# A fused Fourier mixing and hardswish MLP kernel: one difference of VectorE placed behind a block's last output sum, and the second batch's inverse stage in four units of three tiles on another list of steps

## The chip, the cores and the metric

The kernel runs on one core of one Trainium2 chip. The metric is the device time of one execution in microseconds (us). The median of three executions before the change is 2656.8 us (2656.7 to 2656.96). The engines are called as the profile calls them: PE is TensorE's matmuls and PEld its weight loads, DVE is VectorE, ACT is ScalarE, POOL is GpSimd, SP is the engine that issues most DMAs.

## The reference

```python
x: (8, 3008, 256)    filt_r, filt_i: (1505, 256)    w_in: (256, 2048)    w_out: (2048, 256)

X = np.fft.rfft(x, axis=1)
Y = X * (filt_r + 1j * filt_i)[None, :, :]
y = np.fft.irfft(Y, n=3008, axis=1).astype(np.float32)      # mixing along the sequence

t = y.reshape(8 * 3008, 256)                                # 24064 tokens
h = t @ w_in
g = h * np.clip(h + 3.0, 0.0, 6.0) / 6.0                    # hardswish
out = g @ w_out
```

All of it is in float32.

## The kernel before

**Two parts, woven together.** The MLP runs over 47 blocks (`NBLK`) of 512 tokens. A block has eight pairs (`NP`), each for 256 of the 2048 hidden channels. The Fourier mixing runs per batch, as matmuls with tables: 3008 is 47 times 64, and the transform goes through a stage over the 47 (`a_unit`), a stage over the 64 (`b_unit`), the product with the filter (`f_unit`, then the sums in `y_unit`), an inverse stage over the 64 (`bi_unit` or `bi3_unit`), and an inverse stage over the 47 (`n_unit`, `n_five`), which writes the tokens of the coming blocks. Between the stages the data goes through DRAM: `z_tmp` after the first, `g_tmp` after the inverse one, written by `z_store`, `z6_store`, `g_store` and `g3_store` and read back by `t2_load` and `t4_load`. Batch 0 is done ahead; batches 1 to 7 are woven into the MLP of the batch before.

**Steps and the plan.** The loop at the end of the kernel goes through steps i = 8k + p, for block k and pair p. In step i it emits the up half of item i and the down half of item i - 1. The dictionary `plan` says which units of the mixing are emitted in which step, at one of three places: place 0 right behind `up_1`, place 1 behind the first `hswish`, place 2 at the step's end. `at` chooses: `a_unit`, `b_unit`, `bi_unit`, `n_unit` and `n_five` go to place 0 (`EARLY`), `bi3_unit` and `a6_unit` to place 1, all else, `f_unit`, `y_unit` and the stores among them, to place 2. Within one place the order is that of the calls of `at`: those of `n_five` come before those of `b_unit`, and a batch's `y_unit` calls before its `f_unit` calls. The function `places` gives the steps: for batch 1 four lists written out by hand, for the others a regular pattern. The kernel is scheduled by hand: every engine works through its instructions in the order in which this loop emits them.

**A step of the MLP.** The products are done with seven multiplications in place of eight, both up and down. Up (line 764): `up_1` has three products of 256 columns, `up_2` two, `up_3` and `up_5` one each; every matmul shows twice in the profile, as two passes. They go to the PSUM tiles `al` and `be`; ScalarE copies parts out, and VectorE adds them to the two halves of h (`up_2b` line 790, `up_3` line 795). The product of `up_5` goes into the part of `al` that line 795 has read. ScalarE makes relu (line 809), and `hswish` on VectorE (line 814) makes g. The second `hswish` of an item is emitted in the next step, in `g_sums`, ahead of lines 821 and 822, which make the sums G1, G3 and G2. `g_last` (line 827) makes G4. Down (line 843): products 1; then 2 and 4; then 5 and 6; then 7 and 3, each of 128-column matmuls, eight of them in the profile for two products. G4 is used by product 3 alone, the last of a step; 2 and 4 use what the second `hswish` makes, 5 uses G1, 6 G2 and 7 G3.

**Where `g_last` stands.** It comes right behind `g_sums`, or, where `late(i)` holds, behind `up_3`. `late(i)` holds for the second and third step of each block (i % 8 in 1, 2), and where the step before had a heavy unit in the plan (`f_unit`, `y_unit`, sums, `bi3_unit`, `n_five`).

**A block's end.** The eight pairs accumulate in four PSUM banks, `po0` to `po3`. Products 7 and 3 share bank 3, in two halves, and product 7 of pair 0 opens the bank for a new block. In the step of a block's last pair (i % 8 = 0), `out_1` copies a bank on ScalarE, and `out_2` (line 909) and `out_3` (line 914) on VectorE follow, `out_3` behind products 7 and 3 and ahead of place 2. In the next step (i % 8 = 1, the new block's pair 0), `out_4` (lines 918 and 919, and line 920 on GpSimd) and `out_5` (line 923) finish the output. `out_5` reads product 3's half of bank 3; then `store` sends the block out.

**The inverse stage over the 64.** A batch has twelve y tiles (`NU`). `y_unit` makes each one from two products of `f_unit`, which reads a `psF` bank that `b_unit` filled. For batch 1 `b_unit` fills one bank for each y tile; for later batches it fills two at once. `bi_unit` (line 583) takes two y tiles: four matmuls of 512 columns into two `psF` banks, two copies by ScalarE into the tile `t3`, two DMAs on GpSimd's queue (`g_store`, line 630). `bi3_unit` (line 599) takes three: twelve matmuls of 256 columns into two `psF` banks and the PSUM tile `be`; two copies by VectorE (2 and 510 elements, lines 601 and 603) and two by ScalarE (line 602, and line 610 at the end of the step) into `t3`; four DMAs (`g3_store`, lines 615 and 618). Batch 1 uses `bi_unit`, batches 2 to 7 `bi3_unit`.

**Buffers.** `psF` has two banks, shared by `b_unit`, `bi_unit`, `bi3_unit`, `n_unit`, `n_five` (which takes both) and `a6_unit`; `t3` has one buffer, which `a6_unit`, the next batch's first stage, uses too; y tiles three (`yp`), the products of `f_unit` two (`sp`). Five-column chunks of the last stage, `n_five` with 80 matmuls (line 704) and two copies by ScalarE (line 686), stand in steps 17 and 25; its copies set off seven sums of GpSimd (line 760) for the coming block.

Of the kernel before, what the change touches and what calls it, by code (L numbers as in the profile page):

```python
# [39 lines left out]
NB = HC // XC  # L40
# [142 lines left out]
def kernel(  # L183
# [452 lines left out]
    for b in range(B):  # L636
# [4 lines left out]
        n = 0  # L641
# [146 lines left out]
    def up_2b(k, p):  # L788
        al, be, s, s5 = st["up"]
        nc.vector.tensor_tensor(out=st["h"][0].rearrange("p (a n) -> p a n", a=2), in0=be, in1=s, op=ALU.add)  # L790
# [26 lines left out]
    def g_sums(k, p):  # L817
        hswish(k, p, 1)
        g = st["g", k, p]
        v = nc.vector  # L820
        v.tensor_tensor(out=g[:, G1, :], in0=g[:, G3, :], in1=g[:, G22, :], op=ALU.add)  # L821
        v.tensor_tensor(out=g[:, G3:G2 + 1:2, :], in0=g[:, G3:G1 + 1, :],  # L822
                        in1=g[:, G11:G11 + 1, :].broadcast_to([P, 2, 256]), op=ALU.subtract)

    def g_last(k, p):
        g = st["g", k, p]
        nc.vector.tensor_tensor(out=g[:, G4, :], in0=g[:, G12, :], in1=g[:, G2, :], op=ALU.subtract)  # L827
# [42 lines left out]
    def plain_up(p):  # L870
        st["g", 0, p] = gp.tile([P, 7, 256], FP32, name="g")
        st["h"] = [psU.tile([P, 512], FP32, name=n) for n in ("al", "be")]
        for i in range(2):
            for d in range(2):
                nc.tensor.matmul(st["h"][i], w_in[p][:, 2 * d + i, :], xn[:, d, :, 0:PAIRS], start=d == 0, stop=d == 1)  # L875
            relu(i)
            hswish(0, p, i)

    def plain_down(p, tokens=(0, 1)):
        g = st["g", 0, p]  # L880
        if p == 0:
            st["po", 0] = [psO.tile([P, 2, 2, P], FP32, name="po%d" % i) for i in range(2)]
        for t in tokens:
            for u in range(2):
                for i, a in ((0, G11), (1, G12)):
                    nc.tensor.matmul(st["po", 0][t][:, u, :, :].rearrange("p a m -> p (a m)"), g[:, a + t, ts(u, P)],  # L886
                                     w_out[p][:, 2 * i:2 * i + 2, :].rearrange("p j m -> p (j m)"),
                                     start=p == 0 and u == 0 and i == 0, stop=p == NP - 1, skip_group_check=True)
# [14 lines left out]
    def o_at(k, t, d):  # L903
        return st["o", k][0][:, t, :, ts(d, P)]
# [17 lines left out]
    def out_5(k):  # L922
        nc.vector.tensor_tensor(out=o_at(k, 0, 1), in0=st.pop(("po", k))[3][:, 1, :, :], in1=o_at(k, 0, 1), op=ALU.add)
        store(k)
# [20 lines left out]
    def store(k):  # L945
        o = st["o", k][0]
        nc.sync.dma_start(o_d[ds(k * PAIRS, PAIRS)].rearrange("(u p) d -> p u d", p=P), o[:, 1, :, :])
        for u, p, m, b_, j, a in runs(k):
            for h in range(1 if j else 2):
                nc.sync.dma_start(raw(out, b_ * N + row(j, h, a), [[NC * D, m], [1, D]]), o[p:p + m, h, u, :])  # L950
        for b_, r, j, m, na in BACK.get(k, ()):
            to, half = out.offset + (b_ * N + N - j) * D, D // 2
            a0, a1 = ([[D, m], [-NC * D, na], [1, D]], [[NA * D, m], [D, na], [1, D]]) if m > 1 else (
                [[half, 2], [-NC * D, na], [1, half]], [[half, 2], [D, na], [1, half]])
            nc.sync.dma_start(bass.AP(tensor=out.tensor, offset=to, ap=a0),
                              bass.AP(tensor=o_d.tensor, offset=o_d.offset + r * D, ap=a1))
# [18 lines left out]
    def at(step, fn, *a):  # L975
        plan.setdefault((step, 0 if fn in EARLY else 1 if fn in (w_scale, bi3_unit, a6_unit) else 2), []).append((fn, a))

    with tc.manual_schedule():
# [160 lines left out]

        def places(n):  # L1140
            if n == 1:
                return (list(range(2, NB + 2)), [12, 13, 15, 18, 19, 20, 22, 23, 26, 27, 28, 30],
                        [14, 15, 16, 19, 21, 22, 24, 25, 27, 29, 30, 31], [16, 21, 24, 29, 31, 32])
            k = first[n] * NP
            a_at = [k - 7 * NP + i for i in A_AT]
            f_at, y_at, bi_at = ([k - (5 - 2 * r) * NP + i for r in range(2) for i in p]
                                 for p in ((2, 3, 6, 7, 12, 13), (4, 5, 10, 11, 14, 15), (11, 17)))
            return a_at, f_at, y_at, bi_at
# [4 lines left out]
        for n in range(1, B):  # L1153
            a_at, f_at, y_at, bi_at = places(n)
            for c, s in enumerate(a_at):
                at(s, a_unit if n == 1 else a6_unit, n, c)
                at(s, a_sums if n == 1 else a6_sums, n, c)
                at(s, *((z_store, n, c, nc.sync) if n == 1 else (z6_store, n, c)))
                if c >= (3 if n == 1 else 2):
                    at(max(a_at[c - 3 + (n > 1)], s - 6), x_load, n, c)  # L1160
                elif n > 1:
                    at(max(prev[-1 if n == 2 else c - 2], s - 6), x_load, n, c)
            for c in range(NT):
                s = f_at[2 * (c - TB) + (n == 1)] + 1 if c >= TB else a_at[-1] + 1
                at(s, t2_load, n, c)
                s = f_at[2 * (c - FB) + 1] + 1 if c >= FB else a_at[-1 if n > 1 else 3] + 1
                at(s, table_load, n, c)
            for i in range(NU):
                if i % 2 == 0 or n == 1:
                    at(f_at[i], b_unit, n, i)  # L1170
                if n == 1 and i % 2 == 0:
                    at(bi_at[i // 2], bi_unit, n, i)
                    at(bi_at[i // 2], g_store, n, i)
                if n > 1 and i % 3 == 0:
                    at(bi_at[i // 3], bi3_unit, n, i)
                    at(bi_at[i // 3], g3_store, n, i)
                at(y_at[i], y_unit, n, i)
            for i in range(NU):
                at(f_at[i], f_unit, n, i)
            prev = a_at  # L1180
# [5 lines left out]
        def late(i):  # L1186
            return i % NP in (1, 2) or any(fn in HEAVY for place in range(3) for fn, a in plan.get((i - 1, place), ()))

        items = [(k, p) for k in range(NBLK) for p in range(NP)]
        for i in range(len(items) + 1):  # L1190
            up = i < len(items)
            k, p = items[min(i, len(items) - 1)]
            dn = i > 0
            kd, pd = items[i - 1]
            def do(place):
                for fn, a in plan.get((i, place), ()):
                    fn(*a)

            if k == 0:
                plain_up(p)  # L1200
                do(0)
                if dn:
                    plain_down(pd)
                do(1)
                do(2)
                continue
            if not up:
                last_down()
                break
            up_1(k, p)  # L1210
            ends = k == LAST and p == NP - 1
            do(0)
            last_plain = dn and kd == 0
            dn = dn and kd > 0
            if dn:
                g_sums(kd, pd)
                if not late(i):
                    g_last(kd, pd)
                down(kd, pd, 1)
            if up:  # L1220
                up_2(k, p)
            if dn and pd == 0 and kd > 1:
                out_4(kd - 1)
            if up:
                up_2b(k, p)
            if dn:
                down(kd, pd, 2, 4)
                if pd == NP - 1:
                    out_1(kd)
            if up:  # L1230
                up_3(k, p)
                if dn and late(i):
                    g_last(kd, pd)
            if dn:
                down(kd, pd, 5, 6)
            if up:
                up_4(k, p)
            if ends:
                out_1(k)
            if last_plain:  # L1240
                plain_down(pd, (0,))
            if dn and pd == 0 and kd > 1:
                out_5(kd - 1)
            if up:
                hswish(k, p, 0)
                do(1)
            if up:
                up_5(k, p)
            bi3_copies()
            if last_plain:  # L1250
                plain_down(pd, (1,))
                plain_out()
            if dn:
                if pd == NP - 1 or ends:
                    out_2(kd)
                down(kd, pd, 7, 3)
                if pd == NP - 1 or ends:
                    out_3(kd)
            do(2)
# [30 lines left out]
```

## Time and profile before

| | |
|---|---|
| median of 3 executions | 2656.8 us |
| the profiled execution | 2656.55 us, its span 2654.7 us |
| TensorE clock granted | 0.999 on average |
| DMA, mean over the span | 75 GB/s |
| an ordinary step without mixing work | 6.15 us |
| the same with a `b_unit` of batch 1 (line 548) | 7.01 us |

The step starts below are those of the first `up_1` matmul of each step in TensorE's timeline (us from the start of the span). They cover the steps in which batch 1 has its middle stages; batch 1's `a_unit` calls come before, and batch 2's first `a6_unit` comes in step 36.

| step | 12 | 16 | 17 | 18 | 20 | 21 | 24 | 25 | 29 | 31 | 32 | 33 | 34 | 35 |
|---|---|---|---|---|---|---|---|---|---|---|---|---|---|---|
| start | 157.80 | 184.98 | 193.89 | 201.74 | 215.76 | 223.11 | 245.17 | 252.86 | 282.19 | 296.89 | 305.80 | 313.16 | 319.50 | 325.65 |

How to read what follows: a line of the timeline has the start, the length, the engine, the line of the kernel, the operation, what it writes and reads, and how many instructions are merged in it; in brackets is how long the engine was idle before it and what ended that. A group or a wait counts all such instructions of the span. Ends of matmuls are modelled, their starts are not.

### The profile page before, as it was taken

The numbers are of one execution on the slowest core, as the hardware profiler recorded it, in microseconds if no ns is written. First come the engines' busy times: TensorE is split into PE (matmuls) and PEld (weight loads), VectorE is DVE, ScalarE is ACT, GpSimd is POOL, SyncE is SP. The second block draws the span as 40 slices with busy tenths as digits, with TensorE's granted clock in tenths as the row PEclk, the third lists the DMA queues.
The fourth block names the chain that finished last, engine by engine and source line by source line (L and its number), as shares of the span: only waits on it lengthen the run. The fifth ranks groups of instructions, "written<-read, shape, count | busy, mean of one in ns | idle before, by whom it ended". The sixth has DMA issues, their size and how long they took to land.

```text
span 2654.7 us, 54856 instructions
## 1 busy us (share of the span) xinstructions
PE 2638.6 (99%) x21872; PEld 2334.1 (88%) x21872; DVE 2038.2 (77%) x3602; ACT 1298.6 (49%) x2682; POOL 484.3 (18%) x707
## 2 busy tenths in 40 slices
PE   8999999999999999999999999999999999999999
PEld 6688888889889898898988988889888888999998
DVE  7878767887678876788767887688877878766666
ACT  4554454444544444444444544545445444454554
POOL 2242021120211102121021210211112120111110
PEclk9999999999999999999999999999999999999999
DMA  9732234112241133411333112331223321110000
GB/s 248 219 92 71 72 84 115 52 32 82 79 116 52 32 85 81 111 52 36 80 88 104 52 37 80 89 103 52 56 61 88 103 56 48 48 43 22 19 20 25
DMA packets 130646, 198.29 MB, mean 75 GB/s; under 512 B 21538, under 2 KB 97408, under 8 KB 130198
## 3 DMA queue, kind: packets, MB, share of 16 engines
q1 hardware_dynamic: 115165, 150.12, 20.7%
q0 software_dynamic: 14656, 44.16, 6.0%
q8 instruction: 173, 2.83, 0.5%
q14 instruction: 83, 0.68, 0.1%
q10 hardware_dynamic: 569, 0.50, 0.1%
HBM read 122.43 MB, written 83.98 MB: 78 GB/s over the span
## 4 chain that ended last, share of the span: by engine, by line
PE 97%; DVE 2%; DMA 1%; issue 0%; ACT 0%; SPq 0%; POOL 0%; POOLq 0%; DVEq 0%
PE po L843 43%; PE al L764 24%; PE be L764 18%; PE psn L704 2%; PE psf L539 1%; PE psf L480 1%; PE po L886 1%; PE be L599 1%; PE psf L599 1%; PE be L480 1%; PE psf L583 0%; DMA w_all<-in_x_dram 0%; PE al L875 0%; PE be L875 0%; DVE g L814 0%; PE po L548 0%
## 5 line engine op out<-in xcount | busy, mean ns | idle before, releaser
L843 PEld LDWEIGHTS po<-w_all,g 128*128 128x128 f32 x10276 | 1366.4, 191 | 121.1 <-issue 20.3
L843 PE MATMUL po<-w_all,g 128*128 128x128 f32 x10276 | 1396.7, 276 | 1.2 <-DVE g L814 0.6
L809 ACT ACTIVATE r<-h,half_c 128x512 f32<-128x512 f32 x736 | 531.0, 721 | 334.1 <-DVE h L790 322.0
L764 PE MATMUL al<-xt,w_all 128*128 128x256 f32 x2208 | 659.7, 381 | 0.1
L814 DVE SCALAR_TENSOR_TENSOR g<-r,h 128x512 f32<-128x512 f32 x736 | 530.1, 720 | 159.8 <-ACT r L809 144.7
L764 PE MATMUL be<-xt,w_all 128*128 128x256 f32 x1472 | 437.8, 379 | 0.0
L790 DVE TENSOR_TENSOR h<-be,s 128x512 f32<-128x512 f32 x368 | 253.8, 690 | 157.3 <-PE be L764 148.6
L764 PEld LDWEIGHTS al<-xt,w_all 128*128 128x128 f32 x2208 | 335.5, 192 | 1.0 <-issue 0.5
L764 PEld LDWEIGHTS be<-xt,w_all 128*128 128x128 f32 x1472 | 279.8, 190 | 37.8
L760 POOL TENSOR_TENSOR xt<-xn 128x256 f32<-128x256 f32 x184 | 135.9, 757 | 876.7 <-ACT xn L686 842.6
L804 ACT ACTIVATE h<-al 128x256 f32<-128x256 f32 x368 | 141.0, 383 | 299.8 <-PE al L764 299.8
L795 DVE TENSOR_TENSOR h<-al,s 128x256 f32<-128x256 f32 x368 | 156.3, 425 | 157.4 <-PE al L764 154.1
L822 DVE TENSOR_TENSOR g<-g 128x512 f32<-128x512 f32 x367 | 261.3, 712 | 12.6
L785 ACT ACTIVATE s<-al 128x256 f32<-128x256 f32 x368 | 141.1, 383 | 211.9 <-PE al L764 210.4
L764 PE MATMUL al<-xn,w_all 128*128 128x256 f32 x736 | 226.1, 389 | 0.0
L776 ACT ACTIVATE s<-be 128x256 f32<-128x256 f32 x368 | 141.1, 383 | 172.2 <-PE be L764 172.2
L764 PE MATMUL be<-xn,w_all 128*128 128x256 f32 x736 | 218.9, 379 | 0.0
L821 DVE TENSOR_TENSOR g<-g 128x256 f32<-128x256 f32 x367 | 167.5, 456 | 12.6
L775 ACT ACTIVATE s<-al 128x256 f32<-128x256 f32 x368 | 140.8, 383 | 71.7 <-PE al L764 71.7
L764 PEld LDWEIGHTS be<-xn,w_all 128*128 128x128 f32 x736 | 139.9, 190 | 18.9
L827 DVE TENSOR_TENSOR g<-g 128x256 f32<-128x256 f32 x367 | 154.6, 421 | 2.5
L920 POOL TENSOR_TENSOR o<-p,o 128x256 f32<-128x256 f32 x46 | 36.8, 799 | 602.8 <-DVE o L918 557.4
(171 smaller groups left out, 1933.5 us busy)
## 6 DMA issues: line engine op xcount, KB each, us to landing
t<-g_tmp SPq DMA_DIRECT2D x184, 120.0 KB
t<-z_tmp SPq DMA_DIRECT2D x42, 512.0 KB
g_tmp<-t POOLq DMA_DIRECT2D x72, 256.0 KB, 5.5
z_tmp<-t POOLq DMA_DIRECT2D x120, 144.0 KB, 3.4
o_tmp<-o SPq DMA_DIRECT2D x46, 256.0 KB
xs<-in_x_dram SPq DMA_DIRECT2D x60, 192.0 KB
ft<-in_filt_r_dram SPq DMA_DIRECT2D x168, 64.0 KB
ft<-in_filt_i_dram SPq DMA_DIRECT2D x168, 64.0 KB
```

The lines of the kernel that those rows point to most:

```text
L764: nc.tensor.matmul(ps, w_in[p][:, w, :], x, start=start, stop=stop, skip_group_check=True)
L776: nc.scalar.activation(out=s5, in_=be[:, 1, :], func=AXT.Copy)
L785: nc.scalar.activation(out=s[:, 1, :], in_=al, func=AXT.Copy)
L790: nc.vector.tensor_tensor(out=st["h"][0].rearrange("p (a n) -> p a n", a=2), in0=be, in1=s, op=ALU.add)
L795: nc.vector.tensor_tensor(out=st["h"][1][:, 256:512], in0=al, in1=s5, op=ALU.add)
L804: nc.scalar.activation(out=st["h"][1][:, 0:256], in_=al, func=AXT.Copy)
L809: nc.scalar.activation(out=r, in_=st["h"][i], func=AXT.Relu, bias=half_c, scale=1.0 / 6.0)
L814: nc.vector.scalar_tensor_tensor(out=st["g", k, p][:, o:o + 2, :].rearrange("p a n -> p (a n)"), in0=st["r", i], scalar=1.0, in1=st["h"][i ...
L821: v.tensor_tensor(out=g[:, G1, :], in0=g[:, G3, :], in1=g[:, G22, :], op=ALU.add)
L822: v.tensor_tensor(out=g[:, G3:G2 + 1:2, :], in0=g[:, G3:G1 + 1, :], in1=g[:, G11:G11 + 1, :].broadcast_to([P, 2, 256]), op=ALU.subtract)
L827: nc.vector.tensor_tensor(out=g[:, G4, :], in0=g[:, G12, :], in1=g[:, G2, :], op=ALU.subtract)
L843: nc.tensor.matmul(st["po", k][bank][:, part, u, :], g[:, a, ts(u, P)], w_out[p][:, w, :], start=(p == 0 and n in OPENS and u == 0), stop= ...
```

## The change

It has two parts. In the loop, for every pair 0 of a block from the third on (`pd == 0 and kd > 1`), `g_last` is emitted behind `out_5` and no longer behind `up_3`: on VectorE lines 827 and 923 change places. And for batch 1 the six `bi_unit` calls with their `g_store` become four of `bi3_unit` with `g3_store`, so that the stage's matmuls come at place 1 of a step; the lists of steps for `f_unit` (and `b_unit`, which shares its list), `y_unit` and the inverse units are other ones. `f_unit` and `y_unit` no longer share a step, three steps have two `y_unit` calls, and the last inverse unit is in step 34 where it was in 32. The steps of `t2_load` and `table_load` follow from the list of `f_unit`.

```diff
         def places(n):
             if n == 1:
-                return (list(range(2, NB + 2)), [12, 13, 15, 18, 19, 20, 22, 23, 26, 27, 28, 30],
-                        [14, 15, 16, 19, 21, 22, 24, 25, 27, 29, 30, 31], [16, 21, 24, 29, 31, 32])
+                return (list(range(2, NB + 2)), [12, 13, 16, 17, 19, 21, 22, 24, 27, 28, 30, 32],
+                        [14, 15, 18, 20, 20, 23, 26, 26, 29, 31, 31, 33], [20, 26, 31, 34])
...
             for i in range(NU):
                 if i % 2 == 0 or n == 1:
                     at(f_at[i], b_unit, n, i)
-                if n == 1 and i % 2 == 0:
-                    at(bi_at[i // 2], bi_unit, n, i)
-                    at(bi_at[i // 2], g_store, n, i)
-                if n > 1 and i % 3 == 0:
+                if i % 3 == 0:
                     at(bi_at[i // 3], bi3_unit, n, i)
                     at(bi_at[i // 3], g3_store, n, i)
                 at(y_at[i], y_unit, n, i)
...
             if up:
                 up_3(k, p)
-                if dn and late(i):
+                if dn and late(i) and not (pd == 0 and kd > 1):
                     g_last(kd, pd)
...
             if dn and pd == 0 and kd > 1:
                 out_5(kd - 1)
+                g_last(kd, pd)
             if up:
                 hswish(k, p, 0)
                 do(1)
```

`bi3_unit` and its helpers, which batch 1 now calls as the others do:

```python
    def bi3_unit(b, i):
        ys = [st.pop(("y", b, i + v)) for v in range(3)]
        c = psU.tile([P, 512], FP32, name="be")
        banks = [psF.tile([P, 512], FP32, name="psf", tag="f") for ri in range(2)]
        t = t3p.tile([P, 3, 2, D], FP32, name="t3")
...
        nc.scalar.activation(out=to[1], in_=banks[1], func=AXT.Copy)
        nc.vector.tensor_copy(out=to[2][:, 2:512], in_=c[:, 2:512])
...
    def g3_store(b, i):
        t = st.pop(("t3", b, i))
        for v in range(2):
            nc.gpsimd.dma_start(g_d[b, :, :, ds(2 * (i + v), 2), :].rearrange("c ri u d -> c ri (u d)"),
                                t[ts(v, 64), 0:2].rearrange("p ri u d -> p ri (u d)"))
        for u in range(2):
            nc.gpsimd.dma_start(g_d[b, :, :, 2 * (i + 2) + u, :], t[ts(u, 64), 2])
```

## The prediction

> **What bounds the kernel now.** The page first: TensorE has no idle time to speak of, and the chain of waits runs through it for 97% of the span. So nothing that another engine saves counts by itself; what counts is where TensorE is held up, or given fewer instructions.
>
> ```profile
> PE 2638.6 (99%) x21872; PEld 2334.1 (88%) x21872; DVE 2038.2 (77%) x3602; ACT 1298.6 (49%) x2682; POOL 484.3 (18%) x707
> ```
>
> Matmul ends are modelled, so I read starts. In TensorE's timeline an ordinary step begins every 6.15 us (171.82 to 177.97). The last quarter of two steps, up_5 and then products 7 and 3:
>
> ```profile
> 304.47 0.60 PE L764 MATMUL al<-xn,w_all 128*128 128x256 f32 x2
> 304.91 1.05 PE L843 MATMUL po<-w_all,g 128*128 128x128 f32 x8
> 305.80 0.60 PE L764 MATMUL al<-xt,w_all 128*128 128x256 f32 x2
> ...
> 317.99 0.60 PE L764 MATMUL al<-xn,w_all 128*128 128x256 f32 x2
> 318.53 1.13 PE L843 MATMUL po<-w_all,g 128*128 128x128 f32 x8
> 319.50 0.60 PE L764 MATMUL al<-xt,w_all 128*128 128x256 f32 x2
> ```
>
> The first (step 31) takes 305.80 - 304.47 = 1.33 us, the second (step 33, which handles a block's p = 0) 1.51: 0.18 is lost. The list of waits, TensorE's weight loads alone, counts how often (us in total, times, longest):
>
> ```profile
> PEld po L843 <- PE po L843: 10.3, 32, 0.3
> ```
>
> The timeline of step 41 shows on what:
>
> ```profile
> 372.09 0.42 DVE L795 TENSOR_TENSOR h<-al,s 128x256 f32<-128x256 f32 x1 [0.41 <-PE al L764]
> 372.44 0.41 DVE L827 TENSOR_TENSOR g<-g 128x256 f32<-128x256 f32 x1
> 372.77 0.42 DVE L923 TENSOR_TENSOR o<-po,o 128x256 f32<-128x256 f32 x1
> 373.33 1.13 PE L843 MATMUL po<-w_all,g 128*128 128x128 f32 x8
> ```
>
> Product 7 starts 0.14 after out_5 (L923) ends at 373.19. G4 (L827) stands ahead of out_5, though product 3, its only user, comes later still. 32 blocks show this; in a 33rd (485.55) GpSimd slows L827 to 0.94 and the wait is 0.48.
>
> In batch 1's stage (steps 12 to 34, 157.80 to 325.65: 167.85 us, 26.4 over 23 ordinary steps) two of six bi_units stop halfway:
>
> ```profile
> 186.37 1.08 PE L583 MATMUL psf<-y,wi 64*64 64x512 f32 x4
> 187.93 1.07 PE L583 MATMUL psf<-y,wi 64*64 64x512 f32 x4 [0.48 <-DVE s L562]
> ```
>
> They wait for f_unit of the step before (L562, 187.18 to 187.87), which still reads a psF bank. And n_five in step 17, with its copies out:
>
> ```profile
> 195.28 1.38 PE L704 MATMUL psn<-wai,t 48*64 48x47 f32 x80
> 196.71 1.02 ACT L686 ACTIVATE xn<-psn 128x470 f32<-128x470 f32 x2 [0.94 <-PE psn L704]
> ```
>
> **What the Trainium skill says.** *PSUM — Partial Sum Buffer*, "The four PSUM rules": the first matmul of an accumulation group clears the bits of a whole bank, so product 7, which opens bank 3, has to wait for out_5, which reads product 3's half of it. The trace agrees: 0.14 us behind. The same page, "Engine vs sequencer instructions": VectorE's and ScalarE's queues are strictly first in, first out; so a sum ahead of out_5 delays it by its full time. *TensorEngine Tiling (Array Packing)*, "Key Properties": a change of tiling mode drains TensorE. Here a step with tiled matmuls is about 0.19 longer than those matmuls. *SBUF — State Buffer*, "Who interferes with whom": VectorE with two SBUF inputs contends with GpSimd's reads. At 202.03, under GpSimd's sums, L814 took 1.22 us against 0.69.
>
> **Part 1: G4 behind out_5.** Instructions are the same; in 45 blocks two neighbours swap. VectorE's 256-wide sums start 0.34 apart, so out_5 ends 0.33 earlier, at 372.86, 0.47 ahead of the old start of product 7. TensorE needs product 7 at 0.44 after up_5's start (as in step 31), 0.10 to 0.11 earlier than now, so the wait goes, with the restart of 0.07 inside the first product (durations 1.13 and 1.05): 0.18 to 0.19 in all. G4 now ends at 373.18. Product 3 begins four matmuls of 0.111 after product 7, at 373.22 + 0.45 = 373.67, and its weight load some 0.2 ahead, 373.46: late enough by 0.28, twice the 0.14 of a handover. hswish(0) stays where it is. So 32 x 0.185 = 5.9; in the 33rd block one L827 of 0.94 leaves, about 0.5. The other 12 had no wait, as their bi3_unit covers it: 0. Part 1: -6.4 us.
>
> **Part 2, what it removes.** The six bi_units, as excess of their steps over 6.15 (from step starts): 16 and 31 2.76 each, 21, 24 and 29 1.54 each, 32 1.22; 11.36 in all. Four bi3_units cost 1.71 each (step 59: 492.67 to 500.52, 7.85, with nothing else in it): 6.84. Saved 4.5. Steps 20, 23 and 28 are 7.35 where a b_unit alone makes 7.01: y_unit and f_unit fell in one step there and VectorE came late. In the new lists none shares a step: 3 x 0.34 = 1.0 saved. The twelve b_units keep 0.86 each. ScalarE sheds four copies, VectorE gains four of 0.16 and 0.69: neither is the bound.
>
> **What it adds.** Three steps that follow a block's last pair (17, 25, 33) now follow an f_unit in step 16, 24 or 32. There out_3 waits for the end of product 3: at 194.09, 0.20 into step 17, to 194.52. f_unit comes after it, three operations at 2.08, to 2.7 into the next step.
> (a) n_five in 17 and 25 takes both psF banks, one of them that f_unit's. It wants to start at 1.39 (195.28 - 193.89) and starts at 2.77: 1.38 each, 2.8.
> (b) In 17 a b_unit stands behind n_five and wants a bank that the first of two copies must empty: 0.2 handover (196.71 against the end of issue at 196.5), 0.51 copy, 0.1 back: 0.8. Queued behind it are the whole step's TensorE work and f_unit.
> (c) Step 33 has no b_unit or n_five to cover: hswish(1) starts at 2.76 and L795 ends 3.49 later (pitches on VectorE: 0.72, 0.46, 0.61, twice 0.34, 0.61, then 0.42), 6.25; up_5 wants its bank at 4.83 (176.65 - 171.82). With the handover 1.55.
> (d) Step 18 follows an f_unit behind out_5, with GpSimd's seven sums running, pushed later by (a). VectorE's slack is from 0 to a lack of 0.7; I take 0.5.
> (e) Two y_units beside a bi3_unit, in 20, 26, 31: 1.44 more than step 59's one, so hswish(1) starts 2.37 into the next step and ends at 3.06; each next step has a b_unit, which puts product 2 at 3.47. Cost 0, and 0.4 each if that cover were gone.
> (f) g3_store: four issues on GpSimd's queue for two, about 2.4 us each unit (501.75 and 502.84 in the trace), nothing due behind them; the last lies two steps later. t3 has one buffer: in step 36 a6_unit's VectorE copy wants it, 19.4 us after step 34 starts; the last store is issued at 11.4 and at 6.0 to landing done at 17.4. Cost 0. SP's filter and z loads move with their units by a step, ahead of use by four or more: 0.
> Added 2.8 + 0.8 + 1.55 + 0.5 = 5.65; saved 5.5. Part 2: about 0 (+0.1). Both ends: the losses (a) to (d) could be near 0 if some order differs from my reading (-5.5), or twice as dear with VectorE behind for several steps (+5).
>
> **Sum.** -6.4 + 0.1 = -6.3 against the profiled execution's own 2656.55 us (span 2654.7 and 1.85 around it): 2650.25. The median of the runs shown is 0.25 higher: 2650.5.
>
> **Rivals.** R1, the moved stage is as cheap as its instruction count: (a) to (d) don't bite, -6.4 - 5.5: 2645. For it: both waits are argued, not seen at these places. Against: step 16's bi_unit shows the very wait. R2, the stage costs more: VectorE's backlog runs on, +4 more: 2654.5; for it, 25 to 33 keeps VectorE loaded with f, y and copies. R3, G4 becomes the late one: product 3's weights wait where product 7 did, part 1 gives 0: 2657. Against it the 0.28 to spare. R4, slower: the last g3_store lands late. a6_unit's copy in step 36 heads VectorE's first-in first-out queue until t3 is free; beyond a landing time of 6 + 2 us, and some 1 us of cover, each us of it is a us of TensorE. It eats the gain from about 15 us and is over 0.2% slower from 21; at 22 us it gives 2664. Against it, stores of this kind landed in 3.4 us between 300 and 345.
>
> **How the numbers follow.** Forecast 0.56, R1 0.15, R2 0.16, R3 0.08, R4 0.05. Predicted is the forecast's 2650.5. Its own spread, 2647.5 to 2653.5, comes from (d), (c) and the two handovers; the range takes in half of R1 and R2's centre: 2645.5 to 2654.7. 0.2% is 5.3 us, about what a measurement of this kernel tells from no change. Faster by more, below 2651.5: R1 and four fifths of the forecast, 0.60. Within: the rest of it, R2, R3, 0.36. Slower 0.04.
>
> **What would show it.** In TensorE's waits the group with 32 times gone or nearly so, and p = 0 steps 1.33 in their last quarter: part 1. A wait on L827 there: R3. Step 17 some 10.7 us long with a wait on L562 ahead of L704 and one on L686 ahead of L548; the same L562 wait in step 25; step 33 near 7.7: part 2. Those absent: R1. A wait of L483 on a DMA in step 36: R4. The prediction is wrong if p = 0 steps keep their 0.18, or the stage moves by over 3 us either way.

## The result, and the profile after

The changed kernel takes 2651.5 us in the median of 15 executions (2650.9 to 2653.22), the kernel before beside it 2657.08 (15 executions, 2655.45 to 2658.8): 5.6 us less, a ratio of 0.9979 with a 95% interval of 0.9972 to 0.9986. The profiled execution took 2651.86 us, its span is 2650.0. The median lies just on the border, 2651.5, that the prediction drew between a gain of more than 0.2% and one within it.

Where the 4.7 us between the two profiled spans went, by the step starts of TensorE's timeline: step 12 starts at 158.24 in place of 157.80, which is start-up and differs from execution to execution (157.1 to 163.0 in the profiles below); steps 12 to 34 take 168.37 in place of 167.85; all the steps after them 5.6 us less. So the gain of this execution is G4's, in the 30 blocks behind the stage, and the new stage is no cheaper than the old one.

TensorE's busy time on the page, and its list of waits (us in total, times, longest):

```profile
PE 2632.3 (99%) x21920; PEld 2341.8 (88%) x21920; DVE 2046.3 (77%) x3610; ACT 1297.1 (49%) x2678; POOL 485.1 (18%) x711
```

```profile
PE psn L704 <- DVE s L562: 2.0, 2, 1.0
PE po L843 <- DVE g L814: 1.3, 2, 0.8
...
PE psf L548 <- ACT xn L686: 0.7, 1, 0.7
```

The group "PEld po L843 <- PE po L843", 32 waits before, is not in the list of the weight loads any more. In its place stand the waits that the stage makes: n_five twice on f_unit (steps 17 and 25), a b_unit on n_five's copy (17), and, in step 33, product 2 on the second hswish (0.77) and product 5 behind L919 (0.29).

Step 41 in VectorE's and TensorE's timelines:

```profile
373.05 0.42 DVE L795 TENSOR_TENSOR h<-al,s 128x256 f32<-128x256 f32 x1 [0.42 <-PE al L764]
373.39 0.41 DVE L923 TENSOR_TENSOR o<-po,o 128x256 f32<-128x256 f32 x1
373.72 0.42 DVE L827 TENSOR_TENSOR g<-g 128x256 f32<-128x256 f32 x1
...
373.74 0.60 PE L764 MATMUL al<-xn,w_all 128*128 128x256 f32 x2
374.18 1.05 PE L843 MATMUL po<-w_all,g 128*128 128x128 f32 x8
375.07 0.60 PE L764 MATMUL al<-xt,w_all 128*128 128x256 f32 x2
```

out_5 now ends at 373.80, 0.38 ahead of product 7, which starts 0.44 after up_5. The last quarter takes 1.33 us where it took 1.51, and the eight matmuls are back at 1.05.

Step 17, TensorE alone:

```profile
192.96 0.31 PE L704 MATMUL psn<-wai,t 48*64 48x47 f32 x2
194.25 1.37 PE L704 MATMUL psn<-wai,t 48*64 48x47 f32 x78 [0.98 <-DVE s L562]
196.28 1.97 PE L548 MATMUL psf<-t,wf 128*128 128x256 f32 x4 [0.66 <-ACT xn L686]
198.04 1.06 PE L843 MATMUL po<-w_all,g 128*128 128x128 f32 x4
198.89 1.06 PE L764 MATMUL al<-xt,w_all 128*128 128x256 f32 x2
199.75 0.64 PE L764 MATMUL be<-xt,w_all 128*128 128x256 f32 x2
200.23 1.05 PE L843 MATMUL po<-w_all,g 128*128 128x128 f32 x8
```

Both forecast waits are there. What was not forecast: the four matmuls of b_unit then take 1.76 us to the next start, where they take 0.86 in other steps and 0.96 behind the same wait in five_53 (below), the next four 0.85 in place of 0.44, the two after them 0.86 in place of 0.43; from 199.75 on all is as usual. The view by stretches names the cause (us; busy time and instructions of PE, PEld, DVE, ACT and POOL; TensorE's granted clock; DMA):

```profile
193.01:196.42 3.41, 1.78 (x82) 1.53 (x82) 3.28 (x6) 1.14 (x3) 0.00 (x0) 1.00 0.02 5
196.42:199.84 3.42, 3.42 (x11) 2.86 (x12) 0.45 (x2) 0.26 (x1) 2.93 (x5) 0.50 0.00 0
199.84:203.25 3.41, 3.41 (x27) 3.25 (x26) 2.19 (x5) 1.28 (x3) 2.72 (x4) 1.00 0.00 0
```

For 3.41 us TensorE was granted half its clock, right after 3.41 us in which it had been busy for 1.78 only. Step 17 takes 12.20 us, and 10.7 had been worked out.

### The profile page after: what moved, and what is told of

Read it like the earlier page. It is cut to its first block, busy times and chain, and to the rows that moved or that the text cites. A ratio compares the mean times of both kernels' runs of the same rounds, so it can differ in the third digit from the quotient of the medians.

```text
span 2650.0 us, 54958 instructions
## 1 busy us (share of the span) xinstructions
PE 2632.3 (99%) x21920; PEld 2341.8 (88%) x21920; DVE 2046.3 (77%) x3610; ACT 1297.1 (49%) x2678; POOL 485.1 (18%) x711
## 4 chain that ended last, share of the span: by engine, by line
PE 98%; DVE 1%; DMA 1%; ACT 0%; issue 0%; SPq 0%; POOL 0%; POOLq 0%; DVEq 0%; ACTq 0%
PE po L843 44%; PE al L764 24%; PE be L764 18%; PE psn L704 2%; PE psf L539 1%; PE psf L480 1%; PE po L886 1%; PE be L599 1%; PE psf L599 1%; PE be L480 1%; DMA w_all<-in_x_dram 1%; PE al L875 0%; PE be L875 0%; PE psf L548 0%; PE po L548 0%; PE psf L453 0%
## 5 line engine op out<-in xcount | busy, mean ns | idle before, releaser
L843 PEld LDWEIGHTS po<-w_all,g 128*128 128x128 f32 x10276 | 1370.7, 191 | 108.0 <-issue 15.5
L843 PE MATMUL po<-w_all,g 128*128 128x128 f32 x10276 | 1394.4, 276 | 1.6 <-DVE g L814 1.3
L814 DVE SCALAR_TENSOR_TENSOR g<-r,h 128x512 f32<-128x512 f32 x736 | 533.1, 726 | 151.3 <-ACT r L809 135.0
L790 DVE TENSOR_TENSOR h<-be,s 128x512 f32<-128x512 f32 x368 | 253.5, 689 | 152.2 <-PE be L764 143.7
L760 POOL TENSOR_TENSOR xt<-xn 128x256 f32<-128x256 f32 x184 | 142.3, 792 | 921.0 <-ACT xn L686 886.9
L795 DVE TENSOR_TENSOR h<-al,s 128x256 f32<-128x256 f32 x368 | 156.0, 424 | 154.9 <-PE al L764 153.3
L827 DVE TENSOR_TENSOR g<-g 128x256 f32<-128x256 f32 x367 | 159.7, 435 | 2.4
```

The source lines that it names most:

```text
L760: nc.gpsimd.tensor_tensor(out=o, in0=x0, in1=x1, op=op_)
L795: nc.vector.tensor_tensor(out=st["h"][1][:, 256:512], in0=al, in1=s5, op=ALU.add)
L814: nc.vector.scalar_tensor_tensor(out=st["g", k, p][:, o:o + 2, :].rearrange("p a n -> p (a n)"), in0=st["r", i], scalar=1.0, in1=st["h"][i ...
L843: nc.tensor.matmul(st["po", k][bank][:, part, u, :], g[:, a, ts(u, P)], w_out[p][:, w, :], start=(p == 0 and n in OPENS and u == 0), stop= ...
```

## The experiments

Each is given against the kernel before or the changed kernel; medians of the executions, and the steps that it touches from its profile. The kernels of a group ran beside the same executions of the kernel before.

| kernel | median, us | ratio to before, 95% interval |
|---|---|---|
| g4_alone | 2651.73 (21) | 0.9981, 0.9974 to 0.9987 |
| stage_alone | 2657.0 (13) | 1.0, 0.9992 to 1.0008 |
| b_to_18 | 2650.42 (12) | 0.9976, 0.9968 to 0.9985 |
| f_to_15 | 2649.16 (7) | 0.9973, 0.9962 to 0.9983 |
| as_changed | 2651.8 (18) | 0.9981, 0.9974 to 0.9988 |
| f_ahead | 2648.3 (5) | 0.9966, 0.9952 to 0.9979 |
| clean_ahead | 2647.8 (5) | 0.9962, 0.995 to 0.9974 |
| clean_y18 | 2647.7 (5) | 0.9966, 0.9952 to 0.9979 |

**One part at a time.** g4_alone is the kernel before with the edit in the loop only:

```diff
-                if dn and late(i):
+                if dn and late(i) and not (pd == 0 and kd > 1):
                     g_last(kd, pd)
...
                 out_5(kd - 1)
+                g_last(kd, pd)
```

> The G4 part by itself, batch 1's stage as before. Theory (the wait of product 7 on out_5 goes in 33 blocks, 0.185 us each and about 0.5 in one): 6.2 to 6.4 us under the kernel before, and the group of 32 waits of the weight loads gone. Rival (the two parts gain together, and the new lists bring part of the 5.6): less than 5 us under it.

stage_alone is the changed kernel with that edit taken back.

> Batch 1's new lists and three-tile units by themselves, G4 where it was. Theory: the stage saves 5.5 us and loses about 6.5 by the waits in steps 17, 25 and 33 and the lower clock in 17, so 0.5 to 1.5 us over the kernel before. Rival (the stage is cheaper as its instructions are fewer): 2 us or more under it.

g4_alone is 5.1 us under the kernel before, less than either end of the theory's range and at the rival's border; stage_alone moves by 0.1. The steps decide between them: behind step 34 g4_alone is 5.5 us shorter than the kernel before and the changed kernel 5.6, step for step the same to 0.02, stage_alone 0.0. The stage brings next to nothing: steps 12 to 34 of stage_alone are 0.6 us shorter than before (167.27 against 167.85), which its median doesn't show. stage_alone is under its expected range by 0.4: its profile has both waits in step 17, but a clock at 1.0, so step 17 takes 10.66.

What g4_alone gives back shows in its step 26, 7.64 us against 7.11 before. VectorE's timeline there:

```profile
259.72 0.82 DVE L827 TENSOR_TENSOR g<-g 128x256 f32<-128x256 f32 x1
260.47 1.21 DVE L814 SCALAR_TENSOR_TENSOR g<-r,h 128x512 f32<-128x512 f32 x1
261.71 1.10 DVE L571 TENSOR_TENSOR y<-s 64x512 f32<-64x512 f32 x1
262.85 1.11 DVE L572 TENSOR_TENSOR y<-s 64x512 f32<-64x512 f32 x1
```

These take 0.42, 0.69, 0.69 and 0.69 elsewhere. GpSimd runs its sums for the next block, and one of the output, from 257.33 to 264.55. In the kernel before, L827 stood one place earlier and took 0.41; L814, L571 and L572 were slow there too (0.89, 1.11 and 1.10). Behind out_5 L827 starts 0.18 us after a sum of GpSimd's and takes twice as long, and with a slower L814 and the y_unit of this step behind it product 2 of step 26 starts 0.5 us late, held up by its hswish.

The new lists have such a place too, step 18. stage_alone and the kernel five_53 (below; in these steps it is the changed kernel) have the same units there, both at a full clock, and differ in G4's place alone. In five_53 L827 and the L814 behind it took 0.67 and 1.21 us beside GpSimd's sums and step 18 took 6.91; in stage_alone they took 0.41 and 0.88, and step 18 took 6.20. So G4's new place is not free: where GpSimd's sums run and much of VectorE's work follows, it cost 0.5 us in the one kernel and 0.7 in the other.

**Is it the clock, and what lets it fall?** b_to_18 takes the b_unit from behind n_five, f_to_15 takes the f_unit away from in front of it:

```diff
 b_to_18
-  f_at [12, 13, 16, 17, 19, ...]   y_at [14, 15, 18, 20, ...]
+  f_at [12, 13, 16, 18, 19, ...]   y_at [14, 15, 17, 20, ...]
 f_to_15
-  f_at [12, 13, 16, 17, 19, ...]   y_at [14, 15, 18, 20, ...]
+  f_at [12, 13, 15, 17, 19, ...]   y_at [14, 16, 18, 20, ...]
```

> The changed kernel, but the b_unit and f_unit of step 17 in step 18 and the y_unit of 18 in 17, so that no b_unit stands behind n_five. Theory (two waits one after the other in step 17, 0.98 and 0.66 us, let the granted clock fall to a half for 3.4 us, which costs 1.7): only the wait on f_unit is left, the clock stays at 1.0 as in step 25, step 17 takes 9.0 in place of 12.2 us, step 18 7.0 in place of 6.2, 2.4 us under the changed kernel. Rival (the matmuls of step 17 are slow because GpSimd's sums run beside them): they stay slow, at most 0.7 us under it.

> The changed kernel, but the b_unit and f_unit of step 16 in step 15 and the y_unit of 15 in 16, so that n_five in step 17 finds both its banks free; the b_unit behind n_five stays. Theory: the wait on f_unit is gone, the one on n_five's copy stays at 0.7 us; if one wait is too little to lower the clock, step 17 takes 9.3 us and the kernel is 2.7 us under the changed one; if this second wait alone lowers it, 11 us and 1.1 under. Rival (GpSimd's sums slow the matmuls): 1.1 under, at a full clock.

Either way one wait is left, 0.98 or 0.67 us, the granted clock is 1.0 to the end of the products, and the matmuls of step 17 have their usual times although GpSimd's sums run as before. Step 17 takes 8.98 and 9.26 us. So the rival falls. The gains are smaller than expected, 1.1 and 2.3 us in the medians against the changed kernel, in part since step 18 took 7.64 and 6.93 where 7.0 and 6.2 were expected: product 2 starts there 0.5 and 0.65 us late, behind VectorE's hswish. By steps 17 and 18 together the two are 1.8 and 2.2 us shorter than the changed kernel's profile; the other 0.7 of b_to_18's shortfall the steps don't show.

The changed kernel once more, for its profile:

> The changed kernel once more, for its profile and a spread of times. If the fall of the granted clock in step 17 comes with the two waits at every execution, it stands in this profile too and the step takes 12.2 us; if it depends on where the two waits fall in a time window of the chip's own, as the profile of the stage alone (10.7 us at a full clock) suggests, it may be absent, and then the step takes 10.6 to 10.7.

The clock fell in step 17 again, for 3.41 us from 201.10, after a stretch of 3.41 us with 1.77 busy, and the step took 12.2. Here it had fallen once before, in the start-up, at 64.57. But the fall in step 17 doesn't come with every execution. The profile of five_53 below has the same lists and the same two waits:

```profile
191.81 0.31 PE L704 MATMUL psn<-wai,t 48*64 48x47 f32 x2
193.10 1.38 PE L704 MATMUL psn<-wai,t 48*64 48x47 f32 x78 [0.98 <-DVE s L562]
195.13 1.13 PE L548 MATMUL psf<-t,wf 128*128 128x256 f32 x4 [0.66 <-ACT xn L686]
196.09 0.61 PE L843 MATMUL po<-w_all,g 128*128 128x128 f32 x4
```

Here the clock stayed at 1.0: b_unit takes 0.96 to the next start, step 17 10.53. Where the two waits fall tells the executions apart. All changes of the granted clock within a profile stand at whole multiples of 3.413 us from each other, so each profile tells where its stretches of that length begin and end. The one ahead of the fall in as_changed's start-up, the one ahead of its fall in step 17, and the first of five_53's in step 17:

```profile
61.15:64.57 3.42, 1.73 (x16) 0.94 (x9) 3.28 (x6) 1.09 (x2) 0.40 (x1) 1.00 0.88 240
197.69:201.10 3.41, 1.77 (x82) 1.53 (x81) 3.28 (x6) 1.09 (x3) 0.00 (x0) 1.00 0.03 5
```

```profile
190.04:193.46 3.42, 2.44 (x37) 1.88 (x40) 3.24 (x6) 1.55 (x4) 0.00 (x0) 1.00 0.00 0
```

Where the clock fell in step 17, one stretch holds both waits and was busy for 1.77 to 1.80 us. In five_53 the border at 193.46 parts them: the stretches on its two sides were busy for 2.44 and 2.75. In stage_alone, the other profile without the fall, the least busy one in step 17 has 2.43.

The clock fell in step 17 in three of five profiled executions with both waits (this kernel's two, and five_place1), and in no profile where one of the two was taken away or shortened (b_to_18, f_to_15, f_ahead and the two clean ones). Its price is less than the 1.5 us by which step 17 grows, as step 18 then finds VectorE done: steps 17 and 18 together take 18.4 us with the fall and 17.44 in five_53 without, so 1.0 us. The forecast for the two was 10.7 + 6.65 = 17.35. How often it comes is not shown: 7 of the 33 executions of the changed kernel have a mean clock that rounds to 1.000, which a fall of this length excludes, and for the others the mean doesn't tell.

**Bank or backlog?** In five_place1 n_five of step 25 stands behind the first hswish:

```diff
-        plan.setdefault((step, 0 if fn in EARLY
+        plan.setdefault((step, 1 if fn is n_five and step == 25 else 0 if fn in EARLY
```

> The changed kernel, but n_five of step 25 behind the first hswish (place 1) in place of right behind up_1. Theory (VectorE is behind by out_2, out_3 and f_unit, and up_5 has to wait for L795 as in step 33 wherever n_five stands): the wait on the bank goes and one of 1.5 us ahead of up_5 comes, step 25 takes 9.0 to 9.3 us as in the changed kernel (9.0). Rival (the bank is all that it waits for): step 25 takes 7.7.

TensorE in step 25:

```profile
254.99 1.13 PE L843 MATMUL po<-w_all,g 128*128 128x128 f32 x8 [0.77 <-DVE g L814]
255.95 0.60 PE L764 MATMUL al<-xt,w_all 128*128 128x256 f32 x2
256.85 1.16 PE L843 MATMUL po<-w_all,g 128*128 128x128 f32 x8 [0.30 <-DVE o L919]
257.94 1.38 PE L704 MATMUL psn<-wai,t 48*64 48x47 f32 x80
```

The wait on the bank is gone, and its place is taken by one on the second hswish (0.77) and one whose last releaser on VectorE is L919 (0.30); step 25 takes 9.28 us against 9.03. The rival's 7.7 is refuted: VectorE is behind, and TensorE pays at both places. The theory's size holds, but its place doesn't: the waits stand ahead of products 2 and 5, 1.07 us in all, and not ahead of up_5, and step 26 takes 8.55 in place of 7.89. The one execution took 2652.33 us.

f_ahead takes f_unit out from behind out_2 and out_3:

```diff
-        plan.setdefault((step, 0 if fn in EARLY
+        plan.setdefault((step, 3 if fn is f_unit and step in (16, 24, 32) else 0 if fn in EARLY
...
+            do(3)
             if dn:
                 if pd == NP - 1 or ends:
                     out_2(kd)
```

> The changed kernel, but in steps 16, 24 and 32 f_unit stands ahead of out_2 and out_3 on VectorE, so that its bank comes free without waiting for the step's last product. Theory (n_five in 17 and 25 waits for that f_unit alone): its wait falls from 1.3 to 0.2 us in both, step 25 takes 7.9 in place of 9.0, step 17 about 9.4 where the clock stays up; step 33 changes by less than 0.3, as VectorE has the same work to do before L795; 2.3 us under the changed kernel, up to 3.9 with the lower clock gone. Rival (the waits come from VectorE's load as a whole and go elsewhere): less than 1 us under it.

Steps 17, 25 and 33 take 9.39, 7.86 and 7.66 us, as expected (7.76 for the last before). VectorE around the start of step 25 at 249.69, and TensorE's n_five:

```profile
250.54 0.69 DVE L562 TENSOR_TENSOR s<-psf,ft 64x512 f32<-64x512 f32 x1
251.27 0.69 DVE L909 TENSOR_TENSOR o<-po,p 128x512 f32<-128x512 f32 x1
252.06 0.42 DVE L914 TENSOR_TENSOR o<-po,o 128x256 f32<-128x256 f32 x1
252.41 0.68 DVE L814 SCALAR_TENSOR_TENSOR g<-r,h 128x512 f32<-128x512 f32 x1
```

```profile
251.08 1.59 PE L704 MATMUL psn<-wai,t 48*64 48x47 f32 x80
```

f_unit ends 1.54 us into the step in place of 2.7, and the hswish starts at 2.72, where it would have started anyway. VectorE's work is only in another order: what n_five needs comes first, and n_five's own 1.3 us then covers the rest. Step 33 has no such cover and hardly gains. f_ahead is 3.2 us under the changed kernel's 2651.5, where 2.3 was expected, and up to 3.9 without the fall of the clock.

**What beats both.** clean_ahead combines these edits, clean_y18 moves one y_unit more:

```diff
 clean_ahead, as f_ahead and
-  f_at [12, 13, 16, 17, 19, ...]   y_at [14, 15, 18, 20, ...]
+  f_at [12, 13, 15, 18, 19, ...]   y_at [14, 16, 17, 20, ...]
 clean_y18
+  f_at [12, 13, 15, 18, 19, ...]   y_at [14, 16, 18, 20, ...]
```

> The edits that were found, together: f_unit and b_unit of step 16 in 15 and those of 17 in 18, y_unit in 14, 16, 17, and f_unit ahead of out_2 in 24 and 32. Theory: step 17 with n_five alone takes 7.7 us, 25 7.9, 33 7.6; 5 us under the changed kernel, about 2646.5. Rival (the stage's losses are set by VectorE's total work, which is the same): less than 3 us under it.

> As clean_ahead, but the third y_unit in step 18 and not in 17. Theory (in step 17 its two sums run beside GpSimd's, 1.1 us each against 0.7, and hold back hswish(1) for product 2 in step 18 by 0.5 us): that wait goes; the y_unit now shares step 18 with an f_unit and costs 0.34 in step 19; 0.3 us under clean_ahead. Rival (the wait comes from n_five's and b_unit's order): step 18 stays at 7.6, and it is 0.3 us over clean_ahead.

clean_ahead takes 2647.8 us, 3.7 under the changed kernel and 1.3 short of the expected 2646.5. Steps 17, 25 and 33 are as expected (7.71, 7.86, 7.66), but step 18 takes 7.63: a y_unit at the end of step 17 runs beside GpSimd's sums. In clean_y18 that goes (step 18 7.01, step 19 7.36 by the 0.34 of a shared step); its steps 17 to 20 sum to 30.0 us against 30.2, which the times can't tell apart. Both are 0.34 to 0.38% faster than the kernel before. Against the changed kernel the intervals of the ratios just overlap, but each one's slowest execution (2648.69 and 2649.28) is under the fastest of the changed kernel's 33 (2650.12), and the steps say where it comes from.

**What slows G4 in some blocks.** In 12 blocks with n_five early in the step the changed kernel gained 0.10 to 0.15 us, not 0.19. Step 49 in VectorE's, GpSimd's and TensorE's timelines:

```profile
431.70 1.59 POOL L760 TENSOR_TENSOR xt<-xt 128x256 f32<-128x256 f32 x2
...
431.92 0.80 DVE L827 TENSOR_TENSOR g<-g 128x256 f32<-128x256 f32 x1
...
432.37 1.11 PE L843 MATMUL po<-w_all,g 128*128 128x128 f32 x8
433.31 0.60 PE L764 MATMUL al<-xt,w_all 128*128 128x256 f32 x2
```

five_53 moves that n_five:

```diff
+            if five and s1 == 49:
+                s0 = s1 = 53
```

> The changed kernel, but the n_five of step 49 in step 53, so that GpSimd's seven sums no longer run while step 49 makes G4. Theory (G4 behind out_5 is slowed by GpSimd's sums, 0.80 us against 0.42, and product 3 then waits a little for it): L827 takes 0.42 in step 49, and products 7 and 3 there take 0.89 us as in step 41, where they took 0.94. Rival (the 0.05 belongs to the tiled n_five matmuls earlier in the step): gone too, but L827 was not its cause and L827 stays at 0.8.

Now L827 takes 0.42 us (428.30), products 7 and 3 start at 428.75 and the next step at 429.64, 0.89 us later, where it was 0.94. This alone doesn't part the two, since the sums and the tiled matmuls left step 49 together. The profile after does: n_five also stands in steps 105, 153 and 297, at the same place of the step, but L827 took 0.67, 0.73 and 0.42 there, and the last quarter 1.33, 1.33 and 1.32. Of the 30 blocks behind the stage only the 12 with L827 at 0.77 or more take 1.36 to 1.41. And in step 49, of the eight weight loads of products 7 and 3 just the first of product 3 is late: at 432.76, 0.05 after L827 ends. So here product 3 does wait for G4, by 0.05. The one execution took 2649.76 us.

## Why the prediction was right

- **Part 1, mechanism and size.** The wait of product 7 on out_5 is gone in all 33 blocks (why the bank can't be opened earlier, which the prediction put down to its cleared bits, no run here tests), by the forecast 0.18 to 0.19 in 17 of the 30 behind the stage. The term was 6.4 us; the sum over the steps behind step 34 is 5.6, where 5.85 of the 6.4 belonged there. What was mis-sized is L827 beside GpSimd: 0.80 us in blocks with an early n_five, for which 0.42 was taken. The block of step 57 gave 0.71 where 0.5 was taken, which hides part of that. That is luck. R3, product 3 waiting on G4, is real at a quarter of a block's gain, and only there.
- **Part 2, what it removes.** Four bi3_unit steps at 7.86 (three of them) and 7.89, as forecast; the 0.34 of shared steps is gone.
- **(a)** Steps 17 and 25: n_five stops after two matmuls and goes on 2.68 us and 2.72 us into its step, where 2.77 was worked out. Step 25 takes 9.03, the forecast to 0.01.
- **(b)** The b_unit behind n_five finds TensorE idle for 0.66 us and starts 2.03 after n_five's restart. Step 17 without the fall agrees with the forecast: 10.66 and 10.53 against 10.7.
- **(c)** Step 33 takes 7.76; 6.15 + 1.55 = 7.70 was the forecast. VectorE's order is as worked out: L795 ends 6.28 us into the step (6.25 in the forecast) and up_5 starts at 6.40. But TensorE stands for most of the loss earlier, ahead of products 2 and 5 (0.77 and 0.29).
- **(d)** Step 18: 0.5 was taken from a range of 0 to 0.7; it lost 0.05 in the changed kernel, where TensorE at half its clock gave VectorE time, and 0.76 in five_53. The reason given, f_unit with GpSimd's sums beside it, isn't enough: stage_alone has both and lost 0.05 at a full clock. G4's new place makes the difference, and the prediction had no term for it.
- **(e) and (f)** Steps 21, 27 and 32 take 7.01, no wait; step 36 takes 7.88 as before, so the last g3_store is in time and R4 has no part.
- **The step that was missing** is TensorE's clock. The prediction priced the two waits in step 17 as the time that TensorE stands, and nothing for what follows. It costs about 1 us when it happens. The range had room for that. With part 1's shortfall of 0.3 that leads from the -6.3 of the sum to about -5.0; the profiled execution is 4.7 under the one before, with a start-up 0.4 longer.

R2 had the sign of this error, but its mechanism, a VectorE backlog that runs on, isn't what was seen: steps 26 to 31 show no wait. R1 falls, (a) to (c) all bite.

## What to carry to other kernels

When VectorE's queue holds two neighbours of which the first is needed later than the second, swap them: here it gave 5.6 us over 30 blocks. Look at what runs beside the one that moves back: under GpSimd's sums the swap gave less in 12 of these blocks, and took back 0.5 and 0.7 us in two places (step 26 of g4_alone, step 18 of five_53). When units move to other steps, look for what now stands behind a wait on the same queue: an f_unit behind a sum that waits for the step's last product kept a PSUM bank 1.2 us longer, and with it the new lists lost nearly all that the new units saved. And before moving the waiting instruction, ask whether the engine it waits for is behind as a whole; reordering that engine's work helped, moving the waiter didn't.

## What the runs showed of the hardware

TensorE's granted clock fell to 0.50 in step 17 for 3.413 us, after a stretch of the same length in which it was busy for about half the time (1.77 to 1.80 us, most of that with small tiled matmuls). All its changes lie on a grid of 3.413 us: in as_changed the times between them are 17, 2, 38, 1 and 717 times that. Counted on this grid, the 15 falls within the twelve spans, those at the kernels' ends too, all follow a stretch with at most 1.80 us of busy TensorE. Of over 9000 stretches that no fall followed, all but one have 1.88 or more; the one has 1.46 and lies in the last microseconds of f_to_15. Matmul ends are modelled, so the border between 1.80 and 1.88 is an estimate, and how much a small tiled matmul counts stays open. Waits of 1.0 us alone (step 25) or 0.7 us alone (f_to_15) leave at least 2.3 us busy in any stretch of this length, wherever it begins, and the clock stayed up.

The Trainium skill, *TensorE: Matmul & The Clock Gate*, "What's actually happening", gives a clock that is halved after an idle window of 3413 ns, and a window that runs freely, not reset by the kernel. The length, the half and the free-running window agree with these profiles; but no idle window was needed here, a half-busy one was enough.

VectorE's sums with both inputs in SBUF took 1.6 to 2 times as long under parts of GpSimd's sums (L827 0.80 and 0.82 against 0.42, L571 1.10 against 0.69), and those with one input in PSUM did not (L790 at 200.50 in the changed kernel, 0.69, with GpSimd's sum of 200.41 to 201.14 beside it), as the page *SBUF — State Buffer* has it.
